# GpSimd's products of p and v stored with the seven keys innermost

## The chip, the cores and the metric

The kernel runs on one core of a Trainium2 chip. The core has five engines that work at once, each through its own instructions in order: TensorE (PE in the profile; its weight loads are PEld) multiplies matrices into PSUM; VectorE (DVE), ScalarE (ACT) and GpSimd (POOL) work element by element on 128 partitions; SyncE (SP) issues the transfers between HBM and SBUF. They wait for each other by semaphores. The metric is the device time of one execution in microseconds (us), lower is better.

## The reference

Three layers follow each other on 2304 tokens of 512 features. The first is attention with 4 batches, 8 heads, 576 positions and 64 features per head, in two parts whose outputs are added: a full attention on means of four positions, and a local one in which a position sees only the keys less than 4 positions away, so seven keys.

```
mask = np.abs(pos[:, None] - pos[None, :]) < factor      # factor = 4
scores = np.where(mask, scale * np.matmul(q, k.transpose(0, 1, 3, 2)), -1000000000.0)
attn = softmax(scores)
out_local = np.matmul(attn, v)
x = (out_up + out_local)
x = prelu(x @ w_in, alpha) @ w_out                       # d_ff 2048
xn = rmsnorm(x) * rms_g
out = (silu(xn @ w_gate) * (xn @ w_val)) @ w_out2        # d_ff 1536
```

## The kernel before, in words

The tokens are worked on in 12 chunks of 192 positions-and-batches (CW), two of which make a block of 384 columns (BW). The two feed-forward layers run block by block on TensorE with weights and activations split into two half-precision parts: `m1_first` and `m1` for the first one (products at L1371 and L1388), `m2` for the second (L1488 and L1517). Each of their steps goes through ScalarE and VectorE: for m1 the activation and the split (L1375, L1377, L373, L374), for m2 the gate (L1497, L1499, L1502) and the split (L1508, L1509). PSUM has two buffers for the products that wait for this.

Attention is laid between these steps as background tasks. The local attention of chunks 0 to 3 is made with matrix products (`Dense`, `DenseHead`). That of chunks 4 to 11, which the change touches, is made element by element in `local_tasks`: the 128 partitions hold 32 stretches of positions for 4 pairs of heads, and a chunk has 6 units (head j of the pair, two positions t and t+1). For each unit the steps are: the product of q with the seven shifted keys into a tile "prod" of 2 x 7 x 64 = 896 elements (`mul_qk`, L478); its sum over the 64 features into "ls" (`red_qk`, L489); for the whole chunk a softmax over the seven (L506 to L520, tile "lm" beside it); the product of the probabilities with the seven shifted rows of v into "prod" again, 896 elements ordered as position, key, feature (`mul_av`, L526); and the sum over the seven keys into "lo" (`red_av`), made by three adds that all stand at L539: 384 elements (keys 0 to 2 plus 3 to 5), 256 elements (two pairs) and 128 elements into "lo". Transposes and an add of the full attention's output follow (`trans`, L573).

Which engine makes a unit's products is given by the letters "GVGVGV": units 0, 2 and 4 go to GpSimd (nc.gpsimd), units 1, 3 and 5 to VectorE; the sums are all VectorE's. "prod" has two buffers (prod_p), so a unit's product can start only when the sum of the unit before the last is done. The last sum of a chunk is asked for with `av_pool` true in all of them, so the other form of the sum in `red_av`, a reduction over a strided view, isn't used.

The order of all instructions on every engine is made by the kernel itself when it is built: `issue_order` gives each instruction a duration by its form (`cost`), counts VectorE's operations with two SBUF inputs and all of GpSimd's as users of one shared path (`second`), plays the program forward and backward 40 times with priorities from the time left behind each instruction, and fixes the order of the best round. VectorE's cost is 89 ns and 1 ns for 0.96 elements (the larger of output and first input); GpSimd's product costs 148 ns and 1.667 ns for each element where an input is repeated innermost.

Of the kernel before, what the change touches and what calls it, by code (L numbers as in the profile page):

```python
# [13 lines left out]
ALU = mybir.AluOpType  # L14
AX = mybir.AxisListType
# [3 lines left out]
def view(ap, dims, off=0, parts=None):  # L19
    p = list(ap.ap[0]) if parts is None else list(parts)  # L20
    return bass.AP(tensor=ap.tensor, offset=ap.offset + off, ap=[p] + [list(d) for d in dims])
# [234 lines left out]
def kernel(  # L256
# [14 lines left out]
    nc = tc.nc  # L271
    B, H, S, D = q.shape
# [16 lines left out]
    ND = 2 * W + 1  # L289
# [172 lines left out]
    def local_tasks(g, engs, tags=(None, None, None), av_pool=True, o_at=None):  # L462
        b, r0, TL, t0 = place_of(g)
        st = {}
        TP = 2
# [49 lines left out]
        def sm2():  # L515
# [3 lines left out]
            nc.vector.reciprocal(m, m)  # L519
            nc.vector.tensor_tensor(out=s, in0=s, in1=m.unsqueeze(3).to_broadcast([128, 2, T, ND]), op=ALU.mult)  # L520

        def mul_av(i):
            j, t = units[i]
            pr = prod_p.tile([128, TP, ND, D], F32, tag="prod", name="prod")
            st["p", i] = pr
            engs[i].tensor_tensor(  # L526
                out=pr,
                in0=view(st["s"][:, j, t:t + TP], [[ND, TP], [1, ND], [0, D]]),
                in1=view(st["v"][:, j, t:t + TP], [[D, TP], [D, ND], [1, D]]),
                op=ALU.mult,  # L530
            )

        def red_av(i):
            j, t = units[i]
            if i == 0:
                st["o"] = o_at() if o_at else att.tile([128, T, 2, D], F32, tag="lo", name="lo")
            pr = st.pop(("p", i))
            if av_pool:
                add = lambda o, a, c: nc.vector.tensor_tensor(out=o, in0=a, in1=c, op=ALU.add)  # L539
                add(pr[:, :, 0:3], pr[:, :, 0:3], pr[:, :, 3:6])  # L540
                add(pr[:, :, 0:3:2], pr[:, :, 0:3:2], pr[:, :, 1:7:5])
                add(st["o"][:, t:t + TP, j], pr[:, :, 0], pr[:, :, 2])
            else:
                nc.vector.tensor_reduce(out=st["o"][:, t:t + TP, j], in_=pr.rearrange("p t n d -> p t d n"),
                                        axis=AX.X, op=ALU.add)

        def av(i):
            def f():
                if i < len(units):
                    mul_av(i)  # L550
                if i > 0:
                    red_av(i - 1)
            return f
# [1056 lines left out]
    def local(g, mul="GVGVGV", av=True, tags=(None, None, None), **kw):  # L1610
        return local_tasks(g, [V if c == "V" else G for c in mul], tags, av, **kw)
# [134 lines left out]
```

## Time and profile before

| | us |
|---|---|
| median of 3 runs | 968.88 (968.25 to 971.01) |
| the profiled execution | 967.56 |
| its span, first to last instruction | 965.8 |
| TensorE busy | 929.6 |
| VectorE busy | 685.5 |
| ScalarE busy | 481.7 |
| GpSimd busy | 117.5 |

Busy time is the time in which an engine has an instruction under way; a busy TensorE isn't TensorE at its peak, since its products overlap. In the rows, L539 is line 539 of the kernel, "prod<-prod" names what is written and what is read, and x24 the number of instructions; numbers after a bar are busy us and the mean ns of one. A bracket at the end of a row is idle time of the engine just before the instruction, with what ended it.

### The profile page before, as it was taken

The page shows a single profiled execution, that of the slowest core. Times are in us where ns is not written, and L with a number is a line of the kernel's source. Part 1 is how long each engine was busy: PE and PEld are TensorE (multiplying, and loading weights), DVE is VectorE, ACT ScalarE, POOL GpSimd, SP SyncE. Part 2 cuts the span into 40 slices and gives each one's busy share as a digit, 9 for nine tenths or more (in the row PEclk, how much of TensorE's full clock was granted, in tenths as well). Part 3 has the DMA queues.
Part 4 walks back from the last instruction along what each step waited for, and adds up shares of the span by engine and source line. Part 5 has one row for each costly group of instructions (what it writes and reads, how often), then busy time and mean ns, then how long its engine had stood idle before and what let it go on. Part 6 is the DMA issues. An engine that isn't in the chain of part 4 may idle for free.

```text
span 965.8 us, 16581 instructions
## 1 busy us (share of the span) xinstructions
PE 929.6 (96%) x6484; PEld 600.2 (62%) x6484; DVE 685.5 (71%) x1447; ACT 481.7 (50%) x1108; POOL 117.5 (12%) x96
## 2 busy tenths in 40 slices
PE   6978999999999999999999999999999999999998
PEld 4767777799655555565566655555556666555554
DVE  4789996998999978999987899963333442542333
ACT  5999889889864273233575322221322433321322
POOL 1101100201021103333102313210000000000000
PEclk9978999999999999999999999999999999999999
DMA  8886534574302142122122211000000000000000
GB/s 207 253 274 181 161 100 137 197 226 155 128 1 58 52 141 95 44 72 62 45 85 73 82 38 36 22 22 1 20 14 1 1 1 1 1 1 10 24 1 33
DMA packets 53712, 73.80 MB, mean 76 GB/s; under 512 B 22190, under 2 KB 35138, under 8 KB 53634
## 3 DMA queue, kind: packets, MB, share of 16 engines
q1 hardware_dynamic: 53634, 72.74, 24.9%
q8 instruction: 51, 0.84, 0.4%
q14 instruction: 27, 0.22, 0.1%
HBM read 68.01 MB, written 4.72 MB: 75 GB/s over the span
## 4 chain that ended last, share of the span: by engine, by line
PE 67%; DVE 13%; ACT 9%; issue 6%; DMA 5%; POOL 0%; SPq 0%; ACTq 0%; POOLq 0%
PE gps L1488 23%; PE hps L1371 12%; PE acc L1388 12%; PE oacc L1517 11%; DMA out_dram<-ob 4%; DVE prod L539 2%; DVE ls L489 1%; ACT wr L1110 1%; ACT dls L900 1%; DVE prod L526 1%; ACT wr L1113 1%; ACT wi L373 1%; DVE ghl L374 1%; DVE prod L478 1%; DVE hps L1377 1%
## 5 line engine op out<-in xcount | busy, mean ns | idle before, releaser
L1371 PE MATMUL hps<-xt,wi 128*128 128x192 f16 (+1 forms) x1536 | 357.0, 290 | 7.2 <-DVE g L374 3.8
L1488 PE MATMUL gps<-x,w 128*128 128x384 f16 x1728 | 339.0, 326 | 3.3 <-DVE th L1499 3.0
L1388 PE MATMUL acc<-ghl,wo 128*128 128x384 f16 (+1 forms) x960 | 253.8, 310 | 1.7 <-DVE ghl L374 0.6
L1488 PEld LDWEIGHTS <-w 128*128 128x128 f16 x1728 | 169.9, 99 | 118.4 <-issue 5.2
L1517 PE MATMUL oacc<-w,uhl 128*128 128x512 f16 x630 | 191.5, 379 | 2.3 <-ACT ob L1573 1.6
L1371 PEld LDWEIGHTS <-wi 128*128 128x128 f16 x1536 | 149.5, 100 | 59.4 <-issue 7.3
L1388 PEld LDWEIGHTS <-wo 128*128 128x128 f16 x1344 | 129.0, 98 | 61.7 <-issue 4.5
L1377 DVE SCALAR_TENSOR_TENSOR hps<-g,oma,hps 128x192 f32<-128x192 f32 (+1 forms) x128 | 66.0, 516 | 61.3 <-ACT g L1375 61.0
L1497 ACT ACTIVATE th<-gps,tsc 128x384 f32<-128x384 f32 x72 | 41.8, 580 | 132.3 <-PE gps L1488 131.8
L1517 PEld LDWEIGHTS <-uhl 128*128 128x128 f16 x630 | 61.6, 98 | 67.3 <-issue 2.4
L1499 DVE SCALAR_TENSOR_TENSOR th<-th,gps 128x384 f32<-128x384 f32 x72 | 39.6, 550 | 87.8 <-ACT th L1497 87.4
L1375 ACT ACTIVATE g<-hps 128x384 f32<-128x384 f32 x96 | 47.3, 493 | 84.1 <-PE hps L1371 83.5
L1508 ACT ACTIVATE uhl<-gps 128x384 f16<-128x384 f32 x72 | 41.7, 579 | 94.3 <-DVE gps L1502 85.5
L478 POOL TENSOR_TENSOR prod<-cq,ckv 128x896 f32<-128x896 f32 x24 | 54.8, 2284 | 191.6 <-DVE ls L489 50.6
L1388 PE MATMUL acc<-g,wo 128*128 128x384 f16 (+1 forms) x384 | 70.4, 286 | 0.0
L373 ACT ACTIVATE ghl<-hps,grp 128x384 f16<-128x384 f32 (+1 forms) x73 | 42.0, 576 | 51.2 <-DVE hps L1377 48.6
L1509 DVE TENSOR_TENSOR uhl<-gps,uhl 128x384 f16<-128x384 f32 x72 | 45.3, 629 | 28.1 <-ACT uhl L1508 27.8
L526 POOL TENSOR_TENSOR prod<-ls,ckv 128x896 f32<-128x896 f32 x24 | 43.6, 1816 | 163.3 <-DVE lo L539 70.6
L539 DVE TENSOR_TENSOR prod<-prod 128x384 f32<-128x384 f32 (+1 forms) x96 | 59.4, 630 | 4.3 <-POOL prod L526 4.3
L374 DVE SCALAR_TENSOR_TENSOR ghl<-hps,grp,ghl 128x384 f16<-128x384 f32 (+1 forms) x73 | 44.3, 607 | 23.9 <-ACT ghl L373 23.6
L489 DVE TENSOR_REDUCE ls<-prod 128x14 f32<-128x896 f32 x48 | 51.1, 1075 | 0.1
L1110 ACT ACTIVATE wr<-wr 128x768 f32<-128x768 f32 (+1 forms) x48 | 41.8, 877 | 6.2 <-DMA wr<-in_moe_w_out_dram 3.2
(242 smaller groups left out, 1138.9 us busy)
## 6 DMA issues: line engine op xcount, KB each, us to landing
wr<-in_moe_w_out_dram SPq DMA_DIRECT2D x18, 512.0 KB
wr<-in_moe_w_in_dram SPq DMA_DIRECT2D x10, 768.0 KB
wr<-in_moe_w_gate_dram SPq DMA_DIRECT2D x8, 768.0 KB
wr<-in_moe_w_val_dram SPq DMA_DIRECT2D x8, 768.0 KB
ckv<-in_k_dram SPq DMA_DIRECT2D x7, 768.0 KB
ckv<-in_v_dram SPq DMA_DIRECT2D x7, 768.0 KB
wr<-in_moe_w_out_dram SPq DMA_DIRECT2D x20, 256.0 KB
sd<-in_q_dram SPq DMA_DIRECT2D x24, 144.0 KB
```

The costliest lines, as they stand in the source:

```text
L373: nc.scalar.activation(out=hi, in_=src, func=AF.Copy, scale=s)
L374: nc.vector.scalar_tensor_tensor(out=lo, in0=src, scalar=s, in1=hi, op0=ALU.mult, op1=ALU.subtract)
L478: engs[i].tensor_tensor(out=pr, in0=view(st["q"][:, j, t:t + TP], [[D, TP], [0, ND], [1, D]]), in1=view(st["k"][:, j, t:t + TP], [[D, TP], ...
L489: nc.vector.tensor_reduce(out=st["s"][:, j, t:t + TP], in_=st.pop(("p", i)), axis=AX.X, op=ALU.add)
L526: engs[i].tensor_tensor(out=pr, in0=view(st["s"][:, j, t:t + TP], [[ND, TP], [1, ND], [0, D]]), in1=view(st["v"][:, j, t:t + TP], [[D, TP] ...
L539: add = lambda o, a, c: nc.vector.tensor_tensor(out=o, in0=a, in1=c, op=ALU.add)
L1110: nc.scalar.activation(out=hi.bitcast(F32), in_=hi.bitcast(F32), func=AF.Prelu, scale=2.0 ** -112, alpha=2.0 ** 32)
L1371: nc.tensor.matmul(ps[:, j], wi[:, f + j, a, kk * 128:(kk + 1) * 128], x[:, b_, kk, c0:c0 + n], start=(i == 0), stop=(i == 3 * KK - 1))
L1377: nc.vector.scalar_tensor_tensor(out=ps[:, j], in0=g[:, j], scalar=oma[:, f + j:f + j + 1], in1=ps[:, j], op0=ALU.mult, op1=ALU.add)
L1388: nc.tensor.matmul(acc[e], wo_f(f)[:, a, e * 128:(e + 1) * 128], hl[:, b_], start=(f == f0 and i == 0), stop=(f == f1 and i == 2))
L1488: nc.tensor.matmul(ps, w2_t[i0 + f // 3].rearrange("p a (k c) -> p a k c", k=KK)[:, a, kk, (f % 3) * 128:(f % 3 + 1) * 128], xh[:, b_, kk] ...
L1517: nc.tensor.matmul(acc[tt], t[:, a, tt * 128:(tt + 1) * 128], w[:, b_, f % 3], start=(f in first and i == 0), stop=(f in last and i == 2))
```

## The change

GpSimd's product of the probabilities and v is stored with the seven keys innermost (position, feature, key) instead of position, key, feature. The element order in which it computes stays position, key, feature, so that the store goes 7 elements (28 bytes) further with each element, while both inputs are read as before. The sum over the keys of these units becomes one reduction of VectorE over 7 elements that lie together, 896 elements to 128, in the place of the three adds. VectorE's own units keep their layout and their three adds.

```
+        def by_key(i):
+            return engs[i] is nc.gpsimd
+
+        def over(pr, i):
+            return view(pr, [[ND * D, TP], [1, ND], [ND, D]]) if by_key(i) else pr
...
             engs[i].tensor_tensor(
-                out=pr,
+                out=over(pr, i),
                 in0=view(st["s"][:, j, t:t + TP], [[ND, TP], [1, ND], [0, D]]),
                 in1=view(st["v"][:, j, t:t + TP], [[D, TP], [D, ND], [1, D]]),
                 op=ALU.mult,
...
-            if av_pool:
+            if by_key(i):
+                nc.vector.tensor_reduce(out=st["o"][:, t:t + TP, j], in_=view(pr, [[ND * D, TP], [ND, D], [1, ND]]),
+                                        axis=AX.X, op=ALU.add)
+            elif av_pool:
                 add = lambda o, a, c: nc.vector.tensor_tensor(out=o, in0=a, in1=c, op=ALU.add)
```

## Rows read from the trace of the kernel before

**Rows 1.** The page: busy time of each engine, and busy tenths in 40 slices.
```profile
PE 929.6 (96%) x6484; PEld 600.2 (62%) x6484; DVE 685.5 (71%) x1447; ACT 481.7 (50%) x1108; POOL 117.5 (12%) x96
...
PE   6978999999999999999999999999999999999998
...
DVE  4789996998999978999987899963333442542333
```

**Rows 2.** The page: the chain that ended last, by engine.
```profile
PE 67%; DVE 13%; ACT 9%; issue 6%; DMA 5%; POOL 0%; SPq 0%; ACTq 0%; POOLq 0%
```

**Rows 3.** Busy time by stretches: from and to, length, then each engine.
```profile
core 0: us, PE busy (x) PEld busy (x) DVE busy (x) ACT busy (x) POOL busy (x), PEclk, DMA share, GB/s
...
48.00:96.00 48.00, 38.96 (x394) 32.52 (x393) 41.71 (x97) 46.16 (x118) 4.26 (x8) 0.82 0.73 227
...
288.00:336.00 48.00, 45.64 (x268) 26.07 (x266) 48.00 (x98) 15.62 (x31) 8.72 (x4) 1.00 0.15 45
...
384.00:432.00 48.00, 48.00 (x283) 27.87 (x282) 44.71 (x88) 12.90 (x25) 17.97 (x9) 1.00 0.19 58
432.00:480.00 48.00, 45.82 (x286) 27.85 (x284) 47.74 (x93) 19.65 (x49) 14.33 (x6) 1.00 0.16 48
...
645.00:966.00 321.00, 314.28 (x1844) 180.88 (x1841) 119.18 (x218) 93.12 (x170) 0.00 (x0) 1.00 0.03 8
```

**Rows 4.** Products, reductions and adds: shortest, median and longest ns, or busy us and mean.
```profile
L526 POOL TENSOR_TENSOR prod<-ls,ckv x24: 1687/1714/2928, 227.9 to 634.5; 128x896 f32<-128x896 f32 x24
L489 DVE TENSOR_REDUCE ls<-prod x48: 1066/1075/1086, 188.5 to 618.4; 128x14 f32<-128x896 f32 x48
L795 DVE TENSOR_REDUCE qkp<-T x8: 742/752/754, 9.4 to 36.2; 128x144 f32<-128x576 f32 x8
...
L539 DVE TENSOR_TENSOR prod<-prod 128x256 f32<-128x256 f32 x48 | 31.4, 653 | 0.0
L539 DVE TENSOR_TENSOR prod<-prod 128x384 f32<-128x384 f32 x48 | 29.1, 607 | 4.3 <-POOL prod L526 4.3
...
L539 DVE TENSOR_TENSOR lo<-prod 128x128 f32<-128x128 f32 x48 | 18.3, 381 | 0.0
```

**Rows 5.** VectorE in order of time: start us, us, instruction.
```profile
428.37 0.54 DVE L539 TENSOR_TENSOR prod<-prod 128x384 f32<-128x384 f32 x1
428.84 0.60 DVE L374 SCALAR_TENSOR_TENSOR ghl<-hps,grp,ghl 128x384 f16<-128x384 f32 x1
429.37 1.84 DVE L539 TENSOR_TENSOR prod<-prod 128x256 f32<-128x256 f32 x2
...
431.34 0.41 DVE L539 TENSOR_TENSOR prod<-prod 128x256 f32<-128x256 f32 x1
431.68 0.61 DVE L1377 SCALAR_TENSOR_TENSOR hps<-g,oma,hps 128x384 f32<-128x384 f32 x1
...
437.29 0.28 DVE L539 TENSOR_TENSOR lo<-prod 128x128 f32<-128x128 f32 x1
437.49 1.08 DVE L489 TENSOR_REDUCE ls<-prod 128x14 f32<-128x896 f32 x1
438.49 1.08 DVE L478 TENSOR_TENSOR prod<-cq,ckv 128x896 f32<-128x896 f32 x1
```

**Rows 6.** GpSimd in order of time, and its waits: us in all, times, longest.
```profile
428.59 1.88 POOL L526 TENSOR_TENSOR prod<-ls,ckv 128x896 f32<-128x896 f32 x1 [2.63 <-DVE lo L539]
...
POOL prod L526 <- DVE lo L539: 70.6, 16, 10.9
```

**Rows 7.** ScalarE: stores 24 bytes apart (L793), and in a row (L687, L646).
```profile
L793 ACT ACTIVATE T<-tps x16: 661/678/802, 8.2 to 35.5; 128x288 f32<-128x288 f32 x16
...
L687 ACT ACTIVATE aT<-atps x24: 388/407/435, 118.3 to 519.3; 72x288 f32<-72x288 f32 x24
...
L646 ACT ACTIVATE qkT<-qkps x12: 268/279/298, 110.5 to 513.0; 128x144 f32<-128x144 f32 x12
```

**Rows 8.** TensorE in order of time, where it had stood still.
```profile
440.14 0.32 PE L1371 MATMUL hps<-xt,wi 128*128 128x384 f16 x1 [1.19 <-DVE ghl L374]
```

## The prediction

> **What bounds the kernel now.** I read the page's busy shares and slices first: TensorE is busy for 929.6 of 965.8 us and stands at 9 tenths in nearly every slice from the fifth on, while VectorE is as full only up to about the 26th slice, and GpSimd is busy for 117.5 us in all [rows 1]. The chain that ended last says the same: 67% of it lies on TensorE, 13% on VectorE and 0% on GpSimd [rows 2]. Then I asked for the busy time by stretches, because the change lies in one of them: the products of p and v run from 227.9 us to about 640 us [rows 4]. In that part TensorE stands still for little: 48.00 - 45.64 = 2.4 us in 288 to 336, nothing in 384 to 432, 48.00 - 45.82 = 2.2 us in 432 to 480 [rows 3]. VectorE is close to full beside it: 48.00, 44.71 and 47.74 of 48 us [rows 3]. So the reader is to see two engines that are nearly full at once, of which TensorE sets the time, and VectorE takes something from it only in the two stretches where it has no idle time left. One of those stops is in the rows: at 440.14 us TensorE had waited 1.19 us for a VectorE output [rows 8]. After 645 us VectorE works for 119.18 of 321 us and GpSimd not at all [rows 3].
>
> **The change part by part.** There are 8 chunks of 6 units, and units 0, 2 and 4 of a chunk are GpSimd's: 24 products of p and v [rows 4], and as many on VectorE. The change touches those 24 GpSimd units alone.
>
> *The sum on VectorE.* Removed are three adds per unit, 72 in all; added is one reduction per unit, 24 in all. On a full in-order engine what counts is the distance from one start to the next. Where nothing is in the way, the add of 384 elements holds VectorE for 428.84 - 428.37 = 0.47 us, that of 256 for 431.68 - 431.34 = 0.34 us, that of 128 for 437.49 - 437.29 = 0.20 us [rows 5]: together 1.01 us. The new reduction takes 896 elements to 128. Before has one of 896 to 14, 1.075 us long in the median [rows 4], with 438.49 - 437.49 = 1.00 us to the next start [rows 5], and one of 576 to 144 at 0.752 us [rows 4]. The 320 elements more cost 0.323 us, so the time goes by what is read, and ten times the outputs cost nothing that shows. I take 1.00 us. The sum is 24 x (1.00 - 1.01) = -0.24 us of VectorE time: nothing.
>
> *Blocking.* The adds are longer on average than when free: 48 x (0.607 + 0.653 + 0.381) = 78.8 us [rows 4] against 48 x (0.54 + 0.41 + 0.28) = 59.0 us with the durations of free ones [rows 5], so 19.8 us are lost. The rows show to what: a pair of adds starts at 429.37 us and takes 1.84 us, and GpSimd's product runs from 428.59 to 428.59 + 1.88 = 430.47 us [rows 5, 6]. An operation of VectorE with two inputs in SBUF that meets a GpSimd product stands until the product ends. A reduction with one input has not been seen to stand (1.066 to 1.086 us in 48 cases [rows 4]). But the removed adds are not the ones that stand: "prod" has two buffers, GpSimd can start its next product only in the buffer that its own previous unit gives back, and indeed it waits for the last add "lo" 16 times, 70.6 us [rows 6]. When it runs again, its own unit's sum is over, and what it meets are the adds of VectorE's unit in the other buffer, which the change leaves as they are. I take no gain from this; the bound on the other side is that half of the 19.8 us, 9.9 us of VectorE time, goes.
>
> *The product on GpSimd.* Its inputs are read as before; what changes is the store, 28 bytes from one element to the next instead of 4. No GpSimd operation of before stores in this way. The nearest row is on ScalarE: 288 elements stored 24 bytes apart take 0.678 us, and 288 stored in a row take 0.407 us [rows 7], so 0.271 / 288 = 0.94 ns more for each. Added in full, that is 896 x 0.94 = 0.84 us, and the product goes from 1.69 to 2.53 us. The other end is zero: ScalarE needs 0.279 us for 144 elements and 0.407 for 288, so 0.89 ns for each over a fixed 0.15 us, and with the wide store (0.678 - 0.15) / 288 = 1.83 ns for each; GpSimd already takes up to 1.69 / 896 = 1.88 ns for each [rows 4, 7]. If the store is a pace beside the arithmetic and not a charge on top, it is hidden. Below zero nothing speaks for: nothing is read or computed less. I take the hidden end, at 1.7 to 1.8 us, since the two paces are nearly alike, and keep 0.84 us for the range. [...]
>
> *The order.* All instructions are ordered by the planner in the kernel's own code (issue_order). For VectorE it charges 89 ns and n / 0.96: 489 + 356 + 222 = 1067 ns for the three adds and 1022 ns for the reduction, and it counts the adds, not the reduction, as users of the path shared with GpSimd. It charges GpSimd's product as before, 1642 ns, since it looks at the inputs only. So the costs move little, but the planner repeats itself 40 times and keeps the best, and any instruction may come out in another place, also early, where nothing of the change lies. In 48 to 96 alone TensorE stands still for 48.00 - 38.96 = 9.0 us, and its granted clock is 0.82 of full on average, so partly at the lower of its two levels [rows 3]. No row tells the sign. I take zero and, as an estimate, 3 us either way: a third of that idle time.
>
> No DMA is added or moved by hand, and no semaphore wait beyond those of the reduction, which waits for the product as the first add did; behind it on VectorE stand operations that release TensorE's PSUM buffers. In before VectorE stood idle for a GpSimd product for 4.3 us in all, ahead of the adds of 384 [rows 4].
>
> *Sum.* -0.24 us on VectorE, which has cover in TensorE's 48.00 of 48 us in 384 to 432 [rows 3], 0 on GpSimd, 0 for the order: 967.56 us for the profiled execution (span 965.8 us and 1.8 us around it) stays 967.5. The median of the three runs before lies 1.3 us higher, 968.88; I predict 968.9.
>
> **The rivals.** *Slower: the wide store is paid in full.* The mechanism is GpSimd's longer product, in VectorE's queue: either one of its two-input operations stands 0.84 us longer, or the reduction behind it waits 0.84 us longer. Where VectorE has idle time it is absorbed; the stretches 288 to 336 and 432 to 480 have 0.0 and 0.3 us of it and three products of p and v each (of GpSimd's 4 and 6 instructions there), 384 to 432 has 3.3 us and six of them (of 9) [rows 3]. That gives 6 x 0.84 = 5.0 us and 6 x 0.84 - 3.3 = 1.7 us, so 6.7 us: 975.6 us. It decides (2.9 us, see below) from about 0.45 us per product on, where the two full stretches alone give 2.7 us. For it speaks ScalarE's row; against it that GpSimd's pace per element is no faster than ScalarE's wide store. [...] *Faster: VectorE is relieved.* If the 9.9 us went after all, or one instruction in the place of three gave buffers back sooner, the stops of TensorE in the two full stretches could go: 2.4 + 2.2 = 4.6 us, 964.3 us. Against it stands the two-buffer argument. *The order comes out otherwise:* 966 or 972 us. *The change does nothing that shows* is the forecast itself.
>
> **How the numbers follow.** A measurement of this kernel tells about 0.3% (2.9 us) from no change. Forecast, within that bound: 0.50. Wide store paid: 0.22, nearly all of it slower. Relief: 0.10, faster. Another order beyond the bound: 0.10 faster and 0.08 slower. So faster 0.20, same 0.50, slower 0.30. The range reaches from a little past the relief, 963.5, to the wide store, 975.6; the likeliest case alone spans 966 to 972.
>
> **What would show it.** In the profile after: GpSimd's product of p and v at 1.7 to 1.8 us (right) or near 2.5 us (the slower rival); 24 reductions of 896 to 128 at 1.07 to 1.09 us; 72 adds instead of 144, with a mean above that of before, since those that stand remain; VectorE's busy time in the stretches unchanged within 1 us each; TensorE's idle time in 288 to 336 and 432 to 480 still near 2 us. Wrong would be: a reduction that takes longer because it writes more, a product faster than 1.69 us, VectorE's two-input operations standing longer than the product lasts, or a difference that arises before 227 us, where no product of p and v has begun.

## The result and the profile after

The changed kernel takes 975.92 us (median of six runs, 975.14 to 979.39); the kernel before, run beside it, 969.29 us (967.91 to 971.01). The ratio is 1.0072, with a 95% interval of 1.0055 to 1.0089: slower, by more than a measurement of this kernel can leave open. The forecast was no change, and 975.9 us lies 0.3 us above the upper end of the range. The profiled execution after took 975.73 us, with a span of 974.0 us; that of before has 965.8 us, so 8.2 us are to be found.

The page of the kernel after: span, busy time of each engine, VectorE's slices and the chain by engine. The lines answer to [rows 1] and [rows 2].

```profile
span 974.0 us, 16513 instructions
...
PE 932.2 (96%) x6484; PEld 600.2 (62%) x6484; DVE 685.5 (70%) x1399; ACT 480.5 (49%) x1108; POOL 119.0 (12%) x96
...
DVE  4789995898989978999987999962333442442333
...
PE 67%; DVE 15%; ACT 10%; DMA 5%; issue 2%; SPq 0%; ACTq 0%; DVEq 0%
```

VectorE's total is the same to the tenth of a us, 685.5, and GpSimd works for 1.5 us more. TensorE works for 2.6 us more (932.2 against 929.6) and stands still for 5.6 us more. So the cost isn't in the sum of the work that was changed. Tile "prod" in the kernel after (shortest, median and longest ns) and VectorE's groups by form (busy us, mean ns of one) answer to [rows 4]:

```profile
L532 POOL TENSOR_TENSOR prod<-ls,ckv x24: 1815/1835/2642, 228.5 to 635.3; 128x896 f32<-128x896 f32 x24
L532 DVE TENSOR_TENSOR prod<-ls,ckv x24: 1075/1085/2710, 229.7 to 643.0; 128x896 f32<-128x896 f32 x24
L545 DVE TENSOR_REDUCE lo<-prod x24: 1067/1075/1080, 237.6 to 639.8; 128x128 f32<-128x896 f32 x24
```

```profile
L532 DVE TENSOR_TENSOR prod<-ls,ckv 128x896 f32<-128x896 f32 x24 | 35.0, 1458 | 0.0
...
L548 DVE TENSOR_TENSOR prod<-prod 128x384 f32<-128x384 f32 x24 | 17.9, 746 | 0.0
L548 DVE TENSOR_TENSOR prod<-prod 128x256 f32<-128x256 f32 x24 | 16.2, 675 | 0.0
L548 DVE TENSOR_TENSOR lo<-prod 128x128 f32<-128x128 f32 x24 | 8.9, 369 | 0.0
```

GpSimd's product is 0.13 us longer where nothing is in its way (1815 against 1687 ns), the reduction lasts 1.075 us, and 72 adds are gone. Now the stretches. First the kernel before, in those that do not stand in [rows 3], and the part from 228 to 576 us as a whole (from and to, length, then busy us and instructions of each engine, TensorE's granted clock, DMA):

```profile
228.00:288.00 60.00, 58.43 (x453) 40.99 (x451) 56.09 (x118) 47.42 (x68) 9.21 (x5) 1.00 0.26 86
...
336.00:384.00 48.00, 47.34 (x322) 27.73 (x320) 37.70 (x75) 27.76 (x93) 7.12 (x3) 1.00 0.40 129
...
228.00:576.00 348.00, 340.84 (x2240) 209.59 (x2238) 316.78 (x634) 171.85 (x398) 75.53 (x37) 1.00 0.22 71
```

And the kernel after:

```profile
192.00:228.00 36.00, 36.00 (x416) 34.99 (x415) 33.82 (x72) 29.55 (x43) 4.21 (x2) 1.00 0.66 218
228.00:288.00 60.00, 54.56 (x426) 39.31 (x424) 52.76 (x109) 45.78 (x67) 11.36 (x5) 0.97 0.27 88
288.00:336.00 48.00, 47.06 (x278) 26.86 (x278) 48.00 (x91) 18.42 (x34) 7.81 (x4) 1.00 0.15 45
336.00:384.00 48.00, 46.04 (x312) 26.70 (x311) 38.25 (x76) 26.64 (x91) 7.02 (x3) 1.00 0.33 106
384.00:432.00 48.00, 47.97 (x278) 27.33 (x277) 46.17 (x82) 13.57 (x27) 16.69 (x9) 1.00 0.25 82
432.00:480.00 48.00, 45.84 (x284) 27.95 (x282) 47.14 (x73) 12.69 (x25) 14.23 (x7) 1.00 0.12 39
...
228.00:576.00 348.00, 334.95 (x2202) 206.78 (x2200) 314.38 (x589) 171.10 (x398) 75.77 (x36) 1.00 0.23 71
...
645.00:980.00 335.00, 322.41 (x1889) 185.26 (x1887) 122.30 (x224) 94.62 (x173) 0.00 (x0) 1.00 0.03 8
```

The loss is complete when the last product of p and v is done: after 645 us TensorE has 322.41 us of work left where before it had 314.28 [rows 3], 8.1 us more, and nothing is lost behind that. Up to 228 us TensorE is busy for 206.10 us, before for 205.77 us. From 228 to 576 us TensorE stands still for 348 - 334.95 = 13.05 us, where it was 348 - 340.84 = 7.16 us: 5.9 of the 8.2 us. Two thirds of these 5.9 us (60 - 54.56 = 5.44 against 1.57 us) lie in 228 to 288 us alone, where the granted clock is 0.97 instead of 1.00 as well. It is 0.71 from 252 to 256 us and 0.86 from 256 to 260 us: by single us, it stands at 1.00 up to 253 us, at 0.50 from 254 to 257 us, and at 1.00 again from 258 us. (Before has the same two levels in 48 to 96 us: 0.50 from 52 to 58, 62 to 65 and 72 to 78 us, 1.00 from 79 us on.) The 0.50 stands behind 16 us (236 to 252) in which TensorE was busy for 11.8 us: it comes after the stops. I estimate its cost at 0.03 x 60 = 1.8 us. That stretch has five GpSimd instructions, as before. In 288 to 336 and 432 to 480 us, where the prediction looked for the cost, TensorE stands still for 0.94 and 2.16 us, not more than before (2.36 and 2.18).

What TensorE waited for between 228 and 330 us: before, "PE gps L1488 <- DVE th L1499", 2.4 us in three waits; after, the line below (us in all, times, longest), with the longest of these waits and the work that ScalarE had put ahead of the activation "ghl":

```profile
PE acc L1397 <- ACT ghl L373: 4.1, 2, 2.3
```

```profile
241.42 0.92 ACT L1119 ACTIVATE wr<-wr 128x768 f32<-128x768 f32 x1
242.23 0.97 ACT L1122 ACTIVATE wr<-wr,nhalf 128x768 int32<-128x768 uint32 x1
243.11 1.56 ACT L373 ACTIVATE w<-wc,sw 128x1536 f16<-128x1536 f32 x1
244.57 0.56 ACT L373 ACTIVATE ghl<-hps,grp 128x384 f16<-128x384 f32 x1
...
245.19 0.24 PE L1397 MATMUL acc<-ghl,wo 128*128 128x192 f16 x1 [2.31 <-ACT ghl L373]
```

So TensorE waits behind three instructions (0.92 + 0.97 + 1.56 us) that prepare the weights of the second feed-forward layer: none of them belongs to the change. That was the first sign that the instructions' order, not the instructions, had to be tried.

### The profile page after: what moved, and what is told of

It reads as the page before. It is cut to its first block, busy times and chain, and to the rows that moved or that the text cites. A ratio compares the mean times of both kernels' runs of the same rounds, so it can differ in the third digit from the quotient of the medians.

```text
span 974.0 us, 16513 instructions
## 1 busy us (share of the span) xinstructions
PE 932.2 (96%) x6484; PEld 600.2 (62%) x6484; DVE 685.5 (70%) x1399; ACT 480.5 (49%) x1108; POOL 119.0 (12%) x96
## 4 chain that ended last, share of the span: by engine, by line
PE 67%; DVE 15%; ACT 10%; DMA 5%; issue 2%; SPq 0%; ACTq 0%; DVEq 0%
PE gps L1497 22%; PE acc L1397 15%; PE hps L1380 13%; PE oacc L1526 11%; DMA out_dram<-ob 4%; DVE ls L489 2%; ACT wr L1119 1%; DVE prod L532 1%; ACT wr L1122 1%; DVE prod L478 1%; DVE ghl L374 1%; ACT dls L909 1%; DVE hps L1386 1%; ACT wi L373 1%; DVE prod L548 1%
## 5 line engine op out<-in xcount | busy, mean ns | idle before, releaser
L532 POOL TENSOR_TENSOR prod<-ls,ckv 128x896 f32<-128x896 f32 x24 | 47.5, 1977 | 138.1 <-issue 55.1
L489 DVE TENSOR_REDUCE ls<-prod 128x14 f32<-128x896 f32 x48 | 51.1, 1076 | 0.0
L1119 ACT ACTIVATE wr<-wr 128x768 f32<-128x768 f32 (+1 forms) x48 | 41.6, 876 | 2.0 <-DMA sd<-in_k_dram 1.1
L1511 DVE SCALAR_TENSOR_TENSOR gps<-th,kap,gps 128x384 f32<-128x384 f32 x60 | 37.1, 620 | 7.7 <-PE gps L1497 4.7
```

The costliest lines, as they stand in the source:

```text
L489: nc.vector.tensor_reduce(out=st["s"][:, j, t:t + TP], in_=st.pop(("p", i)), axis=AX.X, op=ALU.add)
L532: engs[i].tensor_tensor(out=over(pr, i), in0=view(st["s"][:, j, t:t + TP], [[ND, TP], [1, ND], [0, D]]), in1=view(st["v"][:, j, t:t + TP], ...
L1119: nc.scalar.activation(out=hi.bitcast(F32), in_=hi.bitcast(F32), func=AF.Prelu, scale=2.0 ** -112, alpha=2.0 ** 32)
```

## The experiments

An order can be taken from one kernel and given to another. The planner's result, the plan, is a list of instructions for each engine (us of the plan are the start times by its own charges); written into the kernel as it is, it replaces the search:

```diff
-    for q in best[1].values():
+    for q in fixed_order().values():
```

Theory A says that the order made by the planner costs the time; theory B that the changed operations do (the longer product, one reduction for three adds). Further letters in the expectations are refinements: C, that the place of the sum in VectorE's queue costs the time, against D, the reduction or the longer product; A1, that the new order loses its time in one place, at the stops between 228 and 288 us, against A2, a little everywhere, and A5, that stops which are taken away come back later; A3, that any small change of a charge gives a bad order, against A4 and A6, that only certain changes do; L, M and E are told below. The medians of before beside which the runs were made are 970.08, 969.46, 969.86 and 969.16 us. The last column is TensorE's idle time from 228 to 576 us in the profiled execution (348 us less its busy time).

| kernel | operations | order | median, us | ratio (95%) | idle, us |
|---|---|---|---|---|---|
| before | before | before | 969.3 | 1 | 7.2 |
| changed | changed | changed | 975.9 | 1.0072 (1.0055 to 1.0089) | 13.0 |
| new_ops_old_order | changed | before | 972.0 | 1.0025 (1.0013 to 1.0036) | 9.9 |
| old_ops_new_order | before | changed | 978.7 | 1.0091 (1.0068 to 1.0115) | 14.3 |
| before_gpsimd_1_ns | before | planned with 1 ns more | 975.1 | 1.0059 (1.0044 to 1.0074) | 11.3 |
| before_160_rounds | before | 160 rounds | 971.3 | 1.0022 (1.0005 to 1.0039) | 6.0 |
| planner_45_ns_less | before | planned with 45 ns less | 978.5 | 1.0090 (1.0061 to 1.0119) | 12.1 |
| changed_160_rounds | changed | 160 rounds | 978.9 | 1.0098 (1.0066 to 1.0130) | 8.4 |

### Operations and order apart

**The changed operations in before's order.** The reduction stands where the last of the three adds stood.

> The changed kernel's operations in the order of the kernel before: the planner's result of before is written into the kernel, and each new reduction stands where the last of its three adds stood. Theory A (the planner's other order costs the time, the operations cost nothing): 969 us, within 2 us of before. Theory B (the new operations cost it, in any order: GpSimd's product is 0.13 us longer and VectorE's two-input operations stand longer): 974 to 977 us.

Measured: 971.95 us, 1.0025. With the order kept, two thirds of the loss are gone. What is left, 1.9 us by the medians and 1.3 to 3.5 us by the interval, is what the operations cost in this order.

**Before's operations in the changed kernel's order.** The three adds stand where the reduction stands.

> The operations of before (three adds, products stored in a row) in the order of the changed kernel: the planner's result of the changed kernel is written in, and the three adds follow each other where the reduction stands. Theory A (order): 974 to 977 us. Theory B (operations): 969 us, within 2 us of before.

Measured: 978.68 us, 1.0091. The operations of before, in the new order, are not faster than the changed kernel (the intervals overlap). Their three adds stand in one piece here, which they don't in before's order; a share of the 8.6 us may belong to that, and isn't told apart. The stretch and the wait of the changed kernel come with the order (rows of old_ops_new_order, as above):

```profile
228.00:288.00 60.00, 54.37 (x437) 39.95 (x435) 53.01 (x115) 45.87 (x66) 10.72 (x5) 0.97 0.30 99
```

```profile
PE acc L1388 <- ACT ghl L373: 4.1, 2, 2.3
```

The same 4.1 us, the same clock of 0.97 and nearly the same busy time, with none of the changed operations. In new_ops_old_order, with all of them, the clock is 1.00 and TensorE is busy for 2.3 us more than in the changed kernel:

```profile
228.00:288.00 60.00, 56.89 (x438) 39.73 (x436) 55.24 (x109) 46.03 (x66) 8.86 (x5) 1.00 0.25 80
```

Theory A stands for the larger part, and B is left with the 1.3 to 3.5 us.

**Before, with one number of the planner changed by 1 ns.** Nothing else differs from the kernel before:

```diff
-            return 148 + n * (1.667 if any(list(a.ap)[-1][0] == 0 for a in ins) else 2.104)
+            return 149 + n * (1.667 if any(list(a.ap)[-1][0] == 0 for a in ins) else 2.104)
```

> The operations of before; the planner charges 1 ns more for each GpSimd product (149 in the place of 148). Its own plan ends at 955.2 us in the place of 953.3. Theory A3 (any small shift in the planner's costs throws the order about, and the order of before is one of the good ones): 972 to 980 us. Theory A6 (only shifts that belong to the sums hurt): 969 to 970 us.

Measured: 975.06 us, 1.0059. A charge that is 1 ns higher gives another order, and that order costs nearly what the change costs.

### The place and the parts of the sum

**The reduction where the first of the three adds stood**, all else as in new_ops_old_order.

> As the changed operations in the order of before, but each reduction stands where the first of its three adds stood, so that buffers come back sooner and VectorE may wait for GpSimd's product. Theory A (order): 968 to 970 us, the place of 24 reductions matters little. Theory B (operations): 974 to 977 us, if anything more than with the late place, since every longer product is then waited for.

Measured: 979.71 us, 1.0099. The expectation missed: one instruction per unit, some places earlier in VectorE's queue, turns 972 us into 980 us. Either the reduction or the place does it. Before's kernel, with the same place, tells which:

**Before's operations, with the three adds of each GpSimd unit together where the first stood.**

> The operations of before in its own order, but the three adds of each of GpSimd's units follow each other where the first of them stood: 1 us of VectorE in one piece, and the buffer given back early, with neither the wide store nor the reduction. Theory C (what made the early reduction cost 8 us more than the late one is its place: the piece stands ahead of work that TensorE waits for, and GpSimd's next product starts early and makes VectorE's own product stand): 977 to 980 us. Theory D (it is the reduction or the longer product that is waited for): 969 to 972 us.

Measured: 982.07 us, 1.0120. There is neither a reduction nor a wide store in this kernel, and the reduction at the late place, one piece as well, left 2 us: so it is the place. One instance of what it does is the second product of p and v. First new_ops_old_order_early, then adds_together_early (start, us, instruction):

```profile
230.75 1.09 DVE L545 TENSOR_REDUCE lo<-prod 128x128 f32<-128x896 f32 x1 [0.41 <-POOL prod L532]
...
232.10 2.47 DVE L532 TENSOR_TENSOR prod<-ls,ckv 128x896 f32<-128x896 f32 x1
...
231.91 1.85 POOL L532 TENSOR_TENSOR prod<-ls,ckv 128x896 f32<-128x896 f32 x1 [1.20 <-DMA wr<-in_moe_w_out_dram]
```

```profile
231.14 1.69 POOL L526 TENSOR_TENSOR prod<-ls,ckv 128x896 f32<-128x896 f32 x1 [1.52 <-DMA wr<-in_moe_w_out_dram]
```

The sum gives its buffer back sooner, so GpSimd's next product starts at 231 to 232 us, 7 us ahead of before's (238.64 us; the load named in the brackets is one that it doesn't use), and in the first of the two kernels VectorE's own product stands behind it, 2.47 us instead of 1.08. Here a buffer that comes free sooner moved a collision to another place; it gained nothing. That such collisions make up the whole 8 to 12 us isn't shown.

**The store alone.** The product is stored with the keys innermost, and the three adds stay, in before's order; they then step by 28 bytes:

```diff
             if by_key(i):
-                nc.vector.tensor_reduce(out=st["o"][:, t:t + TP, j], in_=view(pr, [[ND * D, TP], [ND, D], [1, ND]]),
-                                        axis=AX.X, op=ALU.add)
-            elif av_pool:
+                pr = view(pr, [[ND * D, TP], [1, ND], [ND, D]])
+            if av_pool:
```

> Only the store of GpSimd's products with the keys innermost, in the order of before; VectorE keeps its three adds, which now read and write 28 bytes apart. Theory A (order): 969 us, with GpSimd's product at 1.8 us as in the changed kernel, unless the adds get longer. Theory B (the store costs it): 974 to 977 us. If the adds of these units take longer than 0.47, 0.34 and 0.20 us from start to start, that shows in their rows and is a cost of the wide steps on VectorE.

Measured: 979.93 us, 1.0100. It doesn't isolate the store, since the adds of these units became longer too (VectorE in store_alone):

```profile
428.22 0.88 DVE L547 TENSOR_TENSOR prod<-prod 128x384 f32<-128x384 f32 x1 [1.62 <-POOL prod L532]
...
429.51 0.64 DVE L547 TENSOR_TENSOR prod<-prod 128x256 f32<-128x256 f32 x1
...
431.04 0.40 DVE L547 TENSOR_TENSOR lo<-prod 128x128 f32<-128x128 f32 x1
```

They took 0.54, 0.41 and 0.28 us with rows of 64 together [rows 5]: 0.69 us more per unit, 24 x 0.69 = 16.6 us of VectorE time, in a kernel that is 10 us slower than before. The reduction over keys that lie together is what takes this away; the store by itself has no use without it.

### Where in the order it is lost

**Splices.** Each has the changed operations; up to a point of the plan the instructions follow one order, behind it the other. First the splices at 290 us.

> The changed kernel's operations; every instruction that the planner of before starts in its first 290 us (about 300 us of the trace) stands in the order of before, all others in the order of the changed kernel. Theory A1 (the new order loses its time in one place, where the weights of the second layer are prepared, 228 to 288 us): 970 to 972 us. Theory A2 (the new order is a little worse everywhere): half of the loss, 973 to 974 us.

> The changed kernel's operations the other way round: the first 290 us of the plan in the order of the changed kernel, all else in the order of before. Theory A1 (the loss lies in 228 to 288 us): 976 to 978 us. Theory A2 (a little everywhere): 973 to 974 us.

Measured: 976.70 us (1.0072) for before's order first, and 975.62 us (1.0066) for the new order first. The second says that the new order's first 290 us are enough for the whole loss: its row from 228 to 288 us is that of the changed kernel (TensorE busy for 54.56 us, clock 0.97). The first doesn't count against that: it lost its time at the splice itself (TensorE was busy for 42.12 of 48 us from 288 to 336 us), so a splice adds a cost of its own, and only a splice that stays cheap tells something.

**A few stops taken away.** In the changed kernel ScalarE's "ghl" was moved ahead of the weight work shown above, with five other moves on ScalarE and VectorE between 240 and 254 us.

> The changed kernel with its own order but for six instructions, all between 240 and 254 us: two of VectorE's activations (L1386), the two ScalarE halves and the two VectorE halves of the splits that TensorE waits for stand ahead of the weight decoding, of the adds and of a product's wait that they stood behind. Theory A1 (the loss of the new order are these stops of TensorE, 2.3, 1.8, 0.4 and 0.3 us): 971 to 972 us. Theory A5 (the stops only show that ScalarE and VectorE have more to do than TensorE in 228 to 288 us, and the work that is put back stops TensorE later): 975 to 976 us.

Measured: 976.24 us, 1.0065, as without the moves. The wait for "ghl" (4.1 us) is gone, and another is there (six_moves, 236 to 256 us):

```profile
PE allps L349 <- ACT w L1133: 3.8, 2, 3.5
```

TensorE now waits for the weights that ScalarE was kept from. So the stop at 245 us isn't the cause, but the place where a lag comes to light: the second feed-forward layer's weights are late. Three kernels in which the seventh of their splits on VectorE is to be seen, in this order before, after, six_moves:

```profile
248.69 1.82 DVE L374 SCALAR_TENSOR_TENSOR w<-wc,sw,w 128x1536 f16<-128x1536 f32 x1 [0.23 <-ACT w L373]
```

```profile
254.79 1.81 DVE L374 SCALAR_TENSOR_TENSOR w<-wc,sw,w 128x1536 f16<-128x1536 f32 x1
```

```profile
256.89 1.82 DVE L374 SCALAR_TENSOR_TENSOR w<-wc,sw,w 128x1536 f16<-128x1536 f32 x1 [0.50 <-ACT w L373]
```

It starts at 248.06 us in new_ops_old_order (972.0 us) and 249.11 in before_160_rounds (971.3), and at 256.81 in old_ops_new_order (978.7), 255.72 in before_gpsimd_1_ns (975.1) and 254.09 in planner_45_ns_less (978.5). It is a sign, and not the whole loss: store_alone and new_ops_old_order_early, which lose as much in another way, start it at 251.15 and 252.57 us, and the eighth split of the changed kernel is only 1.6 us behind that of before. The loads of these weights, on SyncE's queue, first before and then after:

```profile
208.07 5.30 SPq L1091 DMA_DIRECT2D wr<-in_moe_w_val_dram  x3
213.42 14.68 SPq L1101 DMA_DIRECT2D wr<-in_moe_w_out_dram  x6
```

```profile
214.33 0.37 SPq L1100 DMA_DIRECT2D wr<-in_moe_w_val_dram  x1
214.74 0.94 SPq L1110 DMA_DIRECT2D wr<-in_moe_w_out_dram  x2
221.82 0.38 SPq L1100 DMA_DIRECT2D wr<-in_moe_w_val_dram  x1
```

One part of "w_val" is issued 8 us later, behind "w_out". From this came three theories: L, the loads' order on SyncE makes the weights late; M, the order of ScalarE's and VectorE's work on them does; E, the time was lost before 190 us of the plan.

**Before's order on all engines except SyncE's queue.**

> The changed operations in before's order on all engines but one: the queue of SyncE, which issues the loads, has the changed kernel's order. Theory L (the second layer's weights are prepared late because their loads are issued in another order): 975 to 978 us, the seventh weight split starts at 254 us or later. Theory M (the lag comes from the order of ScalarE's and VectorE's work): near new_ops_old_order, 971 to 973 us, the seventh split at 248 to 249 us.

Measured: 1008.97 us, 1.0405, which no theory expected. The queue waits for buffers that ScalarE and VectorE give back in another order than it asks for them: 33.2 us in six waits for "wc" alone, the longest 12.1 us. Loads and the work on them have to be in step, and one can't be put back without the other. The run shows how dear a queue out of step is, and doesn't tell L from M.

**Earlier splices, new order first**, at 190, 225 and 255 us of the plan.

> The changed operations; the first 190 us of the plan in the changed kernel's order, all that follows in before's. Theories L and M: nothing is lost before that point, 971 to 973 us. Theory E (the new order has lost its time before 190 us of the plan, in what it leaves to be done): 975 to 977 us.

> As new_order_to_190, spliced at 225 us of the plan, behind the loads that are issued in another order and ahead of most of the work on these weights. Theories L and E: 975 to 977 us. Theory M: 971 to 973 us.

> As new_order_to_190, spliced at 255 us of the plan. Theories L, M and E: 975 to 977 us. If the loss arises only behind 255 us, 971 to 973 us.

Measured: 973.69 us (1.0046, 1.0029 to 1.0062), 975.97 us (1.0067, 1.0041 to 1.0094) and 977.73 us (1.0084, 1.0055 to 1.0114); with nothing of the new order it was 972.0 us. By the medians E has about 1.7 of the 4.0 us, and 975.97 - 973.69 = 2.3 us come from instructions planned between 190 and 225 us; the two intervals overlap, so this share is likely and not shown. At 225 us the sum of the loss is there, in a row like that of the kernel after (new_order_to_225; clock 0.97 again):

```profile
228.00:288.00 60.00, 54.55 (x420) 38.95 (x419) 52.31 (x103) 43.99 (x64) 10.15 (x5) 0.97 0.28 86
```

But the stops in it are others. In new_order_to_255, as in the kernel after, TensorE waits for "ghl" for 2.34 and 1.76 us, at 244.47 and 252.16 us; in new_order_to_225 it waits for the weights "w" for 2.68 us at 240.38 us, close behind the splice (225 us of the plan lies near 235 us of the trace), so that the splice may have added its own cost here too. Nor does the run tell L from M, though its expectation says so. The loads that are issued in another order lie ahead of 225 us, but so does much of the work on these weights: in the kernel after, ScalarE makes 17 of its decoding passes (L1119, L1122) from 200 to 235 us and 11 behind that. What the run does show is that a loss of this size can arise without the new order behind 225 us. Between 190 and 225 us of the plan stands one of the 24 GpSimd products that were changed (at 218 us), and none of the 24 reductions (the first is planned at 227 us).

### How far the planner's own end tells the time

**Before's operations, the planner charging 45 ns less for the last add of each GpSimd unit**, which is what it gains by the change (1067 against 1022 ns).

> The operations of before; the planner alone charges 45 ns less for the last add of each of GpSimd's 24 units, which is the difference between its costs of three adds (1067 ns) and of the reduction (1022 ns). It gives another order. Theory A3 (any small shift in the planner's costs throws the order about, and the time with it): not within 1.5 us of before, on either side. Theory A4 (such shifts don't matter, the new order is bad for another reason, as that the reduction is one piece): within 1.5 us of before.

**160 rounds of the planner instead of 40**, with before's operations and with the changed ones.

> The operations of before; the planner repeats itself 160 times in the place of 40 and keeps the best plan, which ends at 952.0 us in the place of 953.3. Theory A3, if the plan's end told the time: 968 us. If the plan's end doesn't tell it and orders scatter: anywhere between 968 and 980 us.

> The changed kernel with 160 rounds of the planner; its plan ends at 949.5 us in the place of 953.5. If the plan's end tells the time: 971 to 972 us, 4 us under the changed kernel. If orders scatter beyond what the plan knows: anywhere between 968 and 980 us. It is also the try for a version that beats both.

Measured: 978.46, 971.26 and 978.94 us. The ends that the planner itself works out are 953.25 us for before, 953.54 for the changed kernel, 956.3 with 45 ns less, 955.2 with 1 ns more, and with 160 rounds 952.0 (before) and 949.5 (changed). The kernel with the earliest planned end is among the slowest measured (it loses its time early: TensorE is busy for 199.75 of the first 228 us, where before it was 205.77), and the two whose ends differ by 0.3 us, before and changed, lie 6.6 us apart. So a repeated search doesn't mend the loss, and no kernel here beats that of before.

## Why the prediction was wrong

**What was right.** The reduction: 1.075 us in the median, 1067 to 1080 ns, as taken from 896 elements read and not from the outputs. VectorE's busy time: 685.5 and 685.5 us, which is in part luck, since the same operations in before's order take 690.8 us. The store: 1815 against 1687 ns, so +0.13 us, at the hidden end (1.7 to 1.8 us), not +0.84. No relief: GpSimd still waits for the last step of the sum (13 times, 44.9 us, against 16 times and 70.6 us in [rows 6]; in new_ops_old_order 16 times and 72.1 us, so the difference comes with the order), and TensorE's idle time did not fall.

**The step that failed** is the term of the order, "I take zero and, as an estimate, 3 us either way". Its mechanism was seen: the planner may move anything, also where nothing of the change lies. Its size was guessed from the idle time in 48 to 96 us, which has nothing to do with it, and it was given 0.18 of the chance outside the bound. Measured, the order alone is worth 975.9 - 972.0 = 4 us with the changed operations, +5.2 us with 1 ns in a charge (975.06 against 969.86) and +8.6 us with the changed kernel's order on before's operations; five plans for before's operations gave 969.5, 971.3, 975.1, 978.5 and 978.7 us. None is faster than that of before. By these plans the term should have stood at 0 to +9 us, and it is the largest one of the sum. The smaller part of the miss is the 1.3 to 3.5 us of the operations in before's order, which the sum has at -0.24 us, covered.

**The slower rival** had the time (975.6 us) and not the mechanism. It wanted 0.84 us more per product and TensorE's new idle time in 288 to 336 and 432 to 480 us; the product got 0.13 us longer, and those two stretches have no more idle time than before. That its figure lies beside the measured one is chance.

**Blocking.** The prediction said that what a GpSimd product meets are VectorE's adds in the other buffer, and that nothing is gained from fewer adds. That was right. In before the 72 adds of GpSimd's units, which were removed (they are told apart by their place in the plan), last 547, 412 and 279 ns in the mean and none of them over 559 ns: they lost nothing. Those of VectorE's own units last 666, 894 and 484 ns, and all of the lost time lies on them. After, it is still there: 24 x (0.746 + 0.675 + 0.369) = 43.0 us against 24 x 1.23 = 29.5 us when free, so 13.4 us, and 24 x (1.458 - 1.075) = 9.2 us on VectorE's own products, which had lost nothing before (1079 ns in the mean): 22.6 us, where it had been 19.8 us. A part went from VectorE's adds to its products, which the prediction didn't say; the order did it, for old_ops_new_order has products of 1463 ns, and new_ops_old_order of 1107 ns. The longest one after, on VectorE, and GpSimd's product of q and the keys beside it:

```profile
439.02 2.71 DVE L532 TENSOR_TENSOR prod<-ls,ckv 128x896 f32<-128x896 f32 x1
...
438.71 2.07 POOL L478 TENSOR_TENSOR prod<-cq,ckv 128x896 f32<-128x896 f32 x1 [5.24 <-DVE lo L548]
```

GpSimd's product ends at 440.78 us, and VectorE's, which began at 439.02 us, lasts 0.95 us beyond that, near the 1.08 us of a free one. It is so in the whole trace: 27 of VectorE's products and adds, all with two inputs and this one among them, began under a GpSimd product, and each ended after it, by 21 to 1050 ns; in before it was 22 of 23, by 145 to 1035 ns. The reductions with one input that began under a GpSimd product stayed at 1076 to 1086 ns (10 of them; in before 8, at 1066 to 1086 ns).

**Expected and not seen:** stretches of VectorE unchanged within 1 us. From 228 to 288 us it is busy for 3.3 us less (52.76 against 56.09); it seems to wait in the lag too. And the mark for a wrong prediction, "a difference that arises before 227 us", was nearly the right question: new_order_to_225 says that most of the cause can lie there, in the order, but the time shows only behind it.

**What stays open.** Of the 4 us between 972.0 and 975.9 us, which instruction in the new order begins the lag: the late loads, the work of ScalarE and VectorE on these weights, which also frees their buffers, or both, isn't told apart: old_order_new_loads put them out of step, and the splice at 225 us takes both along. The 1.3 to 3.5 us that the changed operations take in before's order were not split further. VectorE is busy for 5.3 us more in that run (690.8 against 685.5), but more blocking of the adds doesn't show: those of 256 elements in VectorE's own units last 878 ns there and 894 ns in before. And in old orders the changed operations seem to cost, in the new one to gain (975.9 against 978.7): the intervals overlap there, so nothing is built on it.

## What to carry to other kernels

Where a planner orders the instructions, an edit is two edits: the operations, and a new draw of the order, which in the plans measured here is worth 0 to 9 us and more than the operations. Measure them apart by writing the old order into the new kernel, and the new order into the old one, before a cause is named; a planner's charge changed by 1 ns in the old kernel gives one more draw, and a few of them show how wide it is. A stop that can be moved singly and comes back elsewhere with the same total (4.1 us for "ghl", then 3.8 us for "w") is a lag that began earlier.

## What the runs showed of the hardware

A store of GpSimd that goes 28 bytes further with each element costs 0.128 / 896 = 0.14 ns per element more, where ScalarE's store at 24 bytes cost 0.94 ns, between rows of 128 and 72 partitions [rows 7]: here the price of ScalarE's wide store did not carry over to GpSimd. On VectorE an add of 256 elements that reads and writes at 28 bytes takes 0.64 us instead of 0.41 (store_alone), so 0.9 ns per element, near ScalarE's figure. And a reduction from 896 to 128 elements that reads its seven in a row costs what one from 896 to 14 costs, 1.075 us.
